# Twenty products in the second group, and the range check moved to ScalarE

## The chip, the core and the metric

The kernel runs on one core of one Trainium2 chip. The metric is the device time of one execution in microseconds: the median of several runs. Before the change it is 560.08 us (three runs, 558.29 to 560.13).

## What is computed

Two blocks stand one behind the other. The first is a gated linear attention: for each of 4 batches and 8 heads a 48 x 48 state is decayed and added to along 768 steps. The second is a two-layer network on its 3072 x 384 result, with SiLU between the layers.

```python
# q, k, v, alpha: (4, 8, 768, 48) float32, alpha between 0.8 and 1
for t in range(S):
    state = alpha[:, :, t, :, None] * state + np.einsum('bhd,bhe->bhde', k[:, :, t], v[:, :, t])
    y[:, :, t] = np.einsum('bhd,bhde->bhe', q[:, :, t], state)
x = y.transpose(0, 2, 1, 3).reshape(3072, 384)
h = x @ w_in                          # w_in: 384 x 2048, float64
out = (h / (1 + np.exp(-h))) @ w_out  # w_out: 2048 x 384, float64
```

The weights come as float64 and are turned into float32 on the chip.

## The kernel before, in words

**Chunks and steps.** The sequence is cut into 24 chunks of 128 tokens (6 along the sequence, 4 batches). The main loop runs 25 steps; step s starts chunk s and ends chunk s - 1. From step 8 on a step has four slots: `scores` of chunk s - 1 (q times k, TensorE; copies out by ScalarE at L806 and L809; masked by GpSimd at L813), `products` of chunk s, `quotient` (both VectorE: scans, transposes), and `values` with `states` of chunk s - 1 (TensorE; ScalarE's copy into `xt` at L851).

**Groups.** Four chunks are a group: 512 tokens, six groups in all, numbered 0 to 5. For each group the network is computed in pieces, which are put between the slots. Pieces are of three kinds:

- `enter_plain(grp, h, pair)`: half the tokens of a group (h) by half of w_in's columns (pair), as ordinary products, four pieces each. ScalarE takes SiLU directly from PSUM (L909).
- `enter(grp, pair)`: all tokens of the group by half of w_in's columns, in seven pieces. It does 20 block products where the ordinary way takes 24, out of sums of blocks: sums of w_in (`sums_w`, 23 for each half, kept in `wx` and in place in `w_in`), sums of xt (`sums_x`, 11 for a group, kept in `xc`), and sums of the results on VectorE (L944), for which ScalarE copies products out of PSUM (L936). SiLU comes last, in place (L941).
- `leave(grp, h)`: the product with w_out, seven pieces, with sums of its own on VectorE (L1033, `side_by_side` at L1019, and the results' at L1042, L1074, L1076, L1085).

Before the change groups 0 and 1 enter by `enter_plain`, groups 2 to 5 by `enter`. `leave` of one group is interleaved with the entry of the next. All products of the entries go through three PSUM banks (`ps_m`), those of `leave` through two (`ps_o`), attention's through three (`ps_a`).

**Order.** `fill(step, slot)` runs after each slot. It computes how many pieces are due at this slot, linearly between marks, and runs them. Each engine's instructions are put in order by a scheduling layer; matmuls are kept in the program's order after the start, and so are the instructions marked `keep_in_program_order`. Sums of w_in for half 0 run in `leave(0, 1)`, for half 1 in `leave(1, 0)`, four after each piece.

**The range check.** The method divides by running products of alpha and converts the weights by bit operations, so the kernel checks that alpha is at most 1 and that the exponents of the weights lie in a range, and falls back on a general version if not. The generator `audit` loads each input once more: 9 pieces of alpha (128 x 1024), 12 of w_in, 16 of w_out (8-byte words), all through one buffer `bits` of the pool `look`. SP issues the loads (L675, L677); VectorE takes the maximum, and for weights the minimum too, into `seen` (L685), 65 reductions. A call to the generator reduces the piece in the buffer and issues the next load. It is called in every second slot from step 15, and what is left runs with the last pieces after the main loop. At the end `seen` is reduced to one flag.

The words of the change stand on these lines of before: `audit` L657, `enter_plain` L897, `enter` L917, `done` in `leave` L1050, the list of pieces L1107 to L1136, `go_on` L1141, `fill` L1166.

Of the kernel before, what the change touches and what calls it, by code (L numbers as in the profile page):

```python
# [9 lines left out]
I32 = mybir.dt.int32  # L10
U32 = mybir.dt.uint32
U8 = mybir.dt.uint8
AF = mybir.ActivationFunctionType
ALU = mybir.AluOpType
E = mybir.EngineType
# [340 lines left out]
def quotients(  # L356
# [19 lines left out]
    nc = tc.nc  # L376
# [177 lines left out]
    earlier, later = [(low, 0), (high, 1)], [(low, 1), (high, 0)]  # L554
    ones = consts.tile([128, 1], F32, name="ones")
    gps.memset(ones, 1.0)

    st = [fix.tile([128, NP, 2, D], F32, name=f"st{b}") for b in range(B)]
    for t in st:
# [92 lines left out]


    AW = 1024
    seen = []

    def audit():  # L657


        flat = alpha.rearrange("b h s d -> (b h s d)").rearrange("(p c) -> p c", p=128)  # L660
        todo = [(flat[:, c : c + AW], AW, 0) for c in range(0, flat.shape[1], AW)]
        if wide:
            todo += [(moe_w_in[t * 128 : t * 128 + 128, c : c + 512], 512, 1)
                     for c in range(0, DF, 512) for t in range(NKT)]
            todo += [(moe_w_out[f * 128 : f * 128 + 128, :], HD, 1) for f in range(NFT)]
        for kind in (0, 1):
            n = sum(x[2] == kind for x in todo)
            if n:
                seen.append([fix.tile([128, n], F32, name=f"seen{kind}{i}") for i in range(2)])
        at = [0, 0]  # L670
        for src, n, kind in todo:
            t = late["look"].tile([128, 512, 2], I32, name="bits")
            if kind == 0:
                x = t.rearrange("p n w -> p (n w)")[:, 0:n].bitcast(F32)
                nc.sync.dma_start(x, src)  # L675
            else:
                nc.sync.dma_start(t[:, 0:n, :].rearrange("p n w -> p (n w)"), src.bitcast(I32))  # L677
                x = t[:, 0:n, 1]
            yield
            i = at[kind]  # L680
            at[kind] += 1
            for which, op in ((0, ALU.max), (1, ALU.min)):
                if kind == 1 or which == 0:
                    tc.keep_in_program_order(
                        dve.tensor_reduce(seen[kind][which][:, i : i + 1], x, axis=AX, op=op,  # L685
                                          apply_absolute_value=True))

    xts, xcs = {}, {}

# [198 lines left out]
    def g_tiles(grp, pair):  # L888
        for h in range(2):
            gts[grp, h, pair] = gpool.tile([128, 4, 2, TB], F32, name="g")  # L890
# [6 lines left out]
    def enter_plain(grp, h, pair):  # L897

        if h == 0:
            g_tiles(grp, pair)  # L900
        xt = xts[2 * grp + h]
        for f in range(8 * pair, 8 * pair + 8, 2):
            ps = bank(f // 2 % 3).rearrange("p (e n) -> p e n", e=2)
            for e in range(2):
                for t in range(NKT):
                    pe.matmul(ps[:, e, :], lhsT=w_in[:, t, (f + e) * 128 : (f + e + 1) * 128],
                              rhs=xt[:, t, :], start=(t == 0), stop=(t == NKT - 1))
            q, i = divmod(f, 4)
            act.activation(gts[grp, h, pair][:, i : i + 2, q % 2, :], ps, AF.Silu)  # L909
            if grp == 1 and pair == h == 0:  # L910
                differences(f // 2)
                differences(4 + f // 2)
            if grp > 0 and f % 8 == 6:
                side_by_side(grp, h, pair)
            yield

    def enter(grp, pair):  # L917
        g_tiles(grp, pair)
        halves = [gts[grp, h, pair] for h in range(2)]

        s = [halves[o % 2][:, o // 2] for o in range(8)]
        todo = iter(PRODUCTS)

        def new(i):
            return bank(i).rearrange("p (e n) -> p e n", e=2)

        def add(ps, first=False):
            w, x = next(todo)
            for e in range(2):
                pe.matmul(ps[:, e], lhsT=block_w(w)[:, 2 * pair + e], rhs=block_x(grp, x),  # L930
                          start=(first and e == 0), stop=(e == 1), skip_group_check=True)

        def copy(ps, to=None):
            if to is None:
                to = late["part"].tile([128, 2, TB], F32, name="part")
            act.copy(to, ps)  # L936
            return to

        def silu(h, i):
            x = halves[h][:, i : i + 2]  # L940
            act.activation(x, x, AF.Silu)  # L941

        def tt(to, a, b, op=ALU.add):
            dve.tensor_tensor(to, a, b, op)  # L944

        a, b, c = [new(i) for i in range(3)]
        add(a, True)
        copy(a, s[6])
        add(b, True)
        copy(b, s[2])  # L950
        add(c, True)
        tt(s[6], s[6], copy(c), ALU.subtract)
        yield
        add(a)
        t = copy(a)
        add(b)
        copy(b, s[4])
        add(c)
        copy(c, s[7])
        tt(s[7], s[7], t, ALU.subtract)  # L960
        yield
        add(a)
        copy(a, s[5])
        add(b)
        copy(b, s[3])
        tt(s[5], s[5], s[3])
        add(c)
        copy(c, s[0])
        yield
        add(a)  # L970
        tt(s[4], a, s[4])
        b = new(1)
        add(b, True)
        add(b)
        copy(b, s[1])
        yield
        c = new(2)
        add(c, True)
        tt(s[2], s[2], copy(c), ALU.subtract)
        a = new(0)  # L980
        add(a, True)
        tt(s[6], a, s[6])
        silu(0, 2)
        add(b)
        tt(s[5], copy(b), s[5], ALU.subtract)
        yield
        add(c)
        tt(s[1], c, s[1])
        tt(s[3], s[1], s[3], ALU.subtract)
        a = new(0)  # L990
        add(a, True)
        tt(s[2], a, s[2])
        add(b)
        tt(s[7], b, s[7])
        silu(1, 2)
        yield
        add(c)
        combine(s[1], -1, s[1], -1, s[0])
        tt(s[0], c, s[0])
        silu(0, 0)  # L1000
        a = new(0)
        add(a, True)
        tt(s[3], a, s[3])
        silu(1, 0)
        turn.append(turn.pop(0))
        for h in range(2):
            side_by_side(grp, h, pair)
        yield
# [7 lines left out]
    def side_by_side(grp, h, pair):  # L1016

        x = cells(grp, h, pair, 1, 0)
        dve.tensor_tensor(x, x, cells(grp, h, pair, 1, 1), ALU.add)  # L1019

    def leave(grp, h):
# [26 lines left out]
        steps = iter(range(7))  # L1048

        def done():  # L1050
            if 2 * grp + h in (1, 2):
                sums_w(2 * grp + h - 1, 4 * next(steps) + 4)

        def new(i):
            return out_bank(i, HO)
# [51 lines left out]
    def plain(grp, h, pair):  # L1107
        return (enter_plain(grp, h, pair), 12, 2 * (2 * grp + h) + 2)

    def group(grp):  # L1110
        return [[(enter(grp, pair), 12, GB * grp + GB)] * 7 for pair in range(2)]

    def output(grp):
        return [[(leave(grp, h), 12, GB * grp + GB)] * 7 for h in range(2)]
# [1 line left out]
    def both(x, y):  # L1116
        for i in range(max(len(x), len(y))):
            pieces.extend(x[i : i + 1] + y[i : i + 1])
# [5 lines left out]
    pieces += [plain(1, 0, 0)] * 4 + [(leave(0, 0), 12, GB)] * 7  # L1124
    phases = [len(pieces)]
    pieces += [plain(1, 1, 0)] * 4
    both([(leave(0, 1), 12, GB)] * 7, [plain(1, 0, 1)] * 4 + [plain(1, 1, 1)] * 4)
    phases.append(len(pieces))
    before = output(1)
    for grp in range(2, NG):  # L1130
# [10 lines left out]
    def go_on():  # L1141

        nonlocal done
        next(pieces[done][0], None)
        done += 1

    audits = audit()
    done, bridged = 0, 0
    STEPS = NT + 1
    SLOTS = 4  # L1150
# [15 lines left out]
    def fill(step, slot):  # L1166

        at = step * SLOTS + slot
        if at < marks[0]:
            if at == SLOTS:  # L1170
                next(conv[0])
            elif step >= 1:
                convert(0, (at - SLOTS) * 3 // (marks[0] - SLOTS) + 1)
            return
        i = next(i for i, m in enumerate(marks[1:]) if at < m)
        a, b = [work_at[n] for n in ([0] + phases)[i : i + 2]]
        due = a + (b - a) * (at - marks[i] + 1) / (marks[i + 1] - marks[i])
        if at % 2 == 0 and step > 3 * GB + 2:
            next(audits, None)
        while work_at[done + 1] <= due and pieces[done][2] <= bridged:  # L1180
            convert(0, 3 * (done // 2) + 6)
            convert(1, 3 * (done - 6) // 2)
            go_on()

    for step in range(STEPS):
        if step == 1:
# [28 lines left out]
    while next(audits, 0) is None:  # L1215
        turns += 1
        for _ in range(1 + turns % 2):
            go_on()

    checks = [(least.rearrange("p n j -> p (n j)"), ALU.min, 2.0**-64, ALU.is_gt),  # L1220
              (seen[0][0], ALU.max, 1.0, ALU.is_le)]
    if wide:
        checks += [(seen[1][0], ALU.max, float(1083 << 20), ALU.is_le),
                   (seen[1][1], ALU.min, float(898 << 20), ALU.is_ge)]
    ends = work.tile([128, len(checks)], F32, name="ends")
    for i, (x, op, bound, holds) in enumerate(checks):
        e = ends[:, i : i + 1]
# [71 lines left out]
```

## Time and profile before

| what | value |
|---|---|
| runs | 560.08 us median, 558.29 to 560.13 |
| profiled execution, first to last instruction (span) | 558.1 us |
| its own time outside the span | not given by the page; the fastest run is 0.2 us above the span, the median 2.0 |
| TensorE | 541.4 us busy, 97% |
| VectorE | 445.1 us busy, 80% |
| ScalarE | 208.4 us busy, 37% |
| GpSimd | 75.9 us busy, 14% |
| mean granted TensorE clock | 0.994 |

The page calls TensorE's matmuls PE and its weight loads PEld, VectorE DVE, ScalarE ACT, GpSimd POOL and SyncE SP. A group line gives line, engine, operation, tiles out<-in, shape and count, then after the bar busy time and mean ns of one, then the engine's idle time just before them and what ended most of it. A matmul in float32 is two rows of the trace, so a product of two matmuls is four rows. A waits line reads: engine, what waited, for whom, then total us, times and longest us. In a timeline the columns are start, us, engine, line, operation, and in brackets the idle time before.

### The profile page before, as it was taken

The page shows a single profiled execution, that of the slowest core. Times are in us where ns is not written, and L with a number is a line of the kernel's source. Part 1 is how long each engine was busy: PE and PEld are TensorE (multiplying, and loading weights), DVE is VectorE, ACT ScalarE, POOL GpSimd, SP SyncE. Part 2 cuts the span into 40 slices and gives each one's busy share as a digit, 9 for nine tenths or more (in the row PEclk, how much of TensorE's full clock was granted, in tenths as well). Part 3 has the DMA queues.
Part 4 walks back from the last instruction along what each step waited for, and adds up shares of the span by engine and source line. Part 5 has one row for each costly group of instructions (what it writes and reads, how often), then busy time and mean ns, then how long its engine had stood idle before and what let it go on. Part 6 is the DMA issues. An engine that isn't in the chain of part 4 may idle for free. (4 is left out here: it accounts for less than half of the span.)

```text
span 558.1 us, 12640 instructions
## 1 busy us (share of the span) xinstructions
PE 541.4 (97%) x5026; PEld 488.8 (88%) x5026; DVE 445.1 (80%) x801; ACT 208.4 (37%) x466; POOL 75.9 (14%) x146
## 2 busy tenths in 40 slices
PE   5999999999999999999999999999999999999996
PEld 3788887998899898899999999988998999998996
DVE  5887889974999799997998986998894775857531
ACT  3456643223333243353353353353263341432200
POOL 4100010221211211021021021021121000001000
PEclk9799999999999999999999999999999999999999
DMA  9999861164445525355445654717712122333101
GB/s 218 255 276 177 232 189 40 38 164 108 126 131 136 142 62 134 88 145 157 129 109 142 194 141 115 198 22 179 180 48 84 53 99 95 111 109 106 38 25 32
DMA packets 99220, 70.13 MB, mean 126 GB/s; under 512 B 56272, under 2 KB 88656, under 8 KB 99152
## 3 DMA queue, kind: packets, MB, share of 16 engines
q1 hardware_dynamic: 97232, 65.30, 44.6%
q0 software_dynamic: 1920, 3.93, 2.0%
q8 instruction: 41, 0.67, 0.5%
q14 instruction: 27, 0.22, 0.1%
HBM read 61.34 MB, written 7.86 MB: 124 GB/s over the span
## 5 line engine op out<-in xcount | busy, mean ns | idle before, releaser
L388 PE MATMUL ps_o<-w_out,g 128*128 128x192 f32 x768 | 134.7, 329 | 1.1 <-DVE o L1042 0.9
L388 PEld LDWEIGHTS ps_o<-w_out,g 128*128 128x128 f32 x768 | 125.4, 190 | 5.1 <-DVE o L1042 2.3
L388 PE MATMUL ps_m<-xt,w_in 128*128 128x256 f32 x480 | 113.6, 383 | 1.5 <-ACT xt L851 1.1
L388 PEld LDWEIGHTS ps_m<-xt,w_in 128*128 128x128 f32 x480 | 89.1, 190 | 14.4 <-ACT xt L851 1.6
L388 PE MATMUL ps_o<-wt,g 128*128 128x192 f32 x576 | 99.7, 326 | 0.0
L388 PEld LDWEIGHTS ps_o<-wt,g 128*128 128x128 f32 x576 | 95.1, 190 | 1.6 <-issue 0.2
L388 PE MATMUL ps_m<-xc,w_in 128*128 128x256 f32 x288 | 70.7, 382 | 0.0
L685 DVE TENSOR_REDUCE seen<-bits 128x1 f32<-128x384 int32 (+2 forms) x65 | 42.5, 689 | 24.0 <-DMA bits<-in_moe_w_out_dram 19.6
L388 PEld LDWEIGHTS ps_m<-xc,w_in 128*128 128x128 f32 x288 | 53.6, 190 | 7.0 <-DVE g L944 0.3
L941 ACT ACTIVATE g<-g 128x1024 f32<-128x1024 f32 x32 | 33.0, 1056 | 59.0 <-DVE g L944 59.0
L1033 DVE TENSOR_TENSOR g<-g 128x512 f32<-128x512 f32 x72 | 49.8, 708 | 6.1 <-PE ps_o L388 6.1
L1045 POOL DMA_DIRECT2D out_dram<-o x40 | 22.0, 550 | 223.2 <-DVE o L1042 127.6
L813 POOL TENSOR_SCALAR_AFFINE_SELECT g<-g 64x256 f32<-64x256 f32 x64 | 34.2, 534 | 124.8 <-ACT g L806 105.8
L388 PE MATMUL ps_m<-xc,wx 128*128 128x256 f32 x192 | 50.0, 383 | 1.0 <-DVE xc L586 1.0
L936 ACT COPY g<-ps_m 128x512 f32<-128x512 f32 x64 | 36.5, 588 | 36.5 <-PE ps_m L388 36.4
L388 PEld LDWEIGHTS ps_m<-xc,wx 128*128 128x128 f32 x192 | 35.2, 190 | 5.3 <-ACT u L1064 1.3
L944 DVE TENSOR_TENSOR g<-ps_m,g 128x512 f32<-128x512 f32 x56 | 37.0, 684 | 2.9 <-PE ps_m L388 2.7
L722 DVE TENSOR_TENSOR_SCAN u<-al,one 128x516 f32<-128x516 f32 x24 | 30.0, 1249 | 10.6 <-ACT al L719 10.3
L909 ACT ACTIVATE g<-ps_m 128x512 f32<-128x512 f32 x32 | 19.1, 596 | 42.8 <-PE ps_m L388 42.3
L936 ACT COPY part<-ps_m 128x512 f32<-128x512 f32 x32 | 18.9, 589 | 43.0 <-DVE g L944 21.3
L752 DVE TENSOR_TENSOR_SCAN p<-al,inv 128x516 f32<-128x516 f32 x24 | 29.9, 1246 | 1.0 <-PE ps_a L388 0.4
L388 PE MATMUL ps_a<-g,vn 128*32 128x128 f32 x768 | 27.5, 278 | 1.8 <-POOL g L801 1.7
(126 smaller groups left out, 611.4 us busy)
## 6 DMA issues: line engine op xcount, KB each, us to landing
bits<-in_moe_w_in_dram SPq DMA_DIRECT2D x24, 512.0 KB, 4.8
bits<-in_moe_w_out_dram SPq DMA_DIRECT2D x32, 384.0 KB, 3.1
at<-in_alpha_dram SPq DMA_DIRECT2D x64, 96.0 KB, 2.5
kt<-in_k_dram SPq DMA_DIRECT2D x64, 96.0 KB, 2.5
qt<-in_q_dram SPq DMA_DIRECT2D x64, 96.0 KB, 2.6
bits<-in_alpha_dram SPq DMA_DIRECT2D x9, 512.0 KB, 3.8
out_dram<-o POOLq DMA_DIRECT2D x40, 96.0 KB, 2.4
flips<-turn SPq DMA_DIRECT2D x12, 256.0 KB, 2.4
```

Source lines behind the costliest of these rows:

```text
L388: in_order(nc.tensor.matmul(*args, **kw))
L685: dve.tensor_reduce(seen[kind][which][:, i : i + 1], x, axis=AX, op=op, apply_absolute_value=True))
L722: dve.tensor_tensor_scan(u[:, end - 1 :: -1], sg[:, end:0:-1], one[:, end:0:-1], 0.0, ALU.mult, ALU.add)
L752: dve.tensor_tensor_scan(p[:, 0:end], sg[:, 0:end], iv[:, 0:end], 0.0, ALU.mult, ALU.add)
L813: gps.affine_select(x, x, pattern=[[0, NP], [1, CH]], compare_op=ALU.is_ge, fill=0.0, base=0, channel_multiplier=-1)
L909: act.activation(gts[grp, h, pair][:, i : i + 2, q % 2, :], ps, AF.Silu)
L936: act.copy(to, ps)
L941: act.activation(x, x, AF.Silu)
L944: dve.tensor_tensor(to, a, b, op)
L1033: dve.tensor_tensor(cells(grp, h, pair, *to), cells(grp, h, pair, *x), cells(grp, h, pair, *y), ALU.subtract)
L1045: (gps if grp < NG - 1 else nc.sync).dma_start(out[r : r + C, c * HO : (c + 1) * HO], o)
```

## The change

- In group 1, half 1 of w_in's columns enters by `enter` (20 products) and no longer by two `enter_plain`; `sums_x(1)` is put ahead of it, and it is interleaved with `leave(0, 1)`. Half 0 of group 1 stays plain.
- For that, half 1's sums of w_in run sooner: three after each piece of `leave(0, 0)` once the late buffers are there, four after each piece of `enter_plain(1, 1, 0)`, the rest at the beginning of `enter`. Half 0's run later, in `leave(1, 0)`, and group 2 takes half 1 first.
- `side_by_side` of the plain pieces (sums of g for `leave`) is put on a list and runs one piece later.
- The range check is done by ScalarE: loads are issued on ScalarE's queue; alpha takes two passes (Abs, then Relu of |x| - 1 with its sum into `beyond`), the weights three (Abs of the upper 16 bits, scaled; Abs of 1 minus that; Relu with its sum). One buffer, as before. The generator is called twice in each slot from step 10 on: first pass ahead of the slot's pieces; the other passes and the next load behind them.
- The check covers the pieces of the weights that are not yet fetched when its list is made: 8 of w_in and 16 of w_out, with the 9 of alpha 33, where it was 37.

```diff
@@ audit @@
-        for src, n, kind in todo:
-            t = late["look"].tile([128, 512, 2], I32, name="bits")
-            ...
-                nc.sync.dma_start(t[:, 0:n, :].rearrange("p n w -> p (n w)"), src.bitcast(I32))
-                x = t[:, 0:n, 1]
-            yield
-            ...
-                        dve.tensor_reduce(seen[kind][which][:, i : i + 1], x, axis=AX, op=op,
-                                          apply_absolute_value=True))
+        def step(to, x, func, scale=1.0, bias=0.0, to_sum=None):
+            kw = {} if to_sum is None else {"accum_out": to_sum}
+            tc.keep_in_program_order(act.activation(to, x, func, bias=bias, scale=scale, **kw))
+
+        def begin(kind, src, n):
+            t = late["look"].tile([128, 512, 2], I32, name="bits")
+            ...
+            tc.keep_in_program_order(act.dma_start(to, src))
+            return t
+
+        t = begin(*audited[0])
+        yield
+        for i, (kind, _, n) in enumerate(audited):
+            ...
+            if kind == 0:
+                step(x, x, AF.Abs)
+            else:
+                step(x, t.bitcast(I16)[:, 0:n, 3], AF.Abs, scale=2.0**-14)
+            yield
+            if kind == 1:
+                step(x, x, AF.Abs, scale=-1.0, bias=ones)
+            step(x, x, AF.Relu, scale=1.0 if kind == 0 else 2.0**14 / 944, bias=minus,
+                 to_sum=beyond[:, i : i + 1])
+            if i + 1 < len(audited):
+                t = begin(*audited[i + 1])
+            yield
@@ enter_plain @@
+            if grp == h == 1:
+                sums_w(1, sums_done[1] + 4)
             if grp > 0 and f % 8 == 6:
-                side_by_side(grp, h, pair)
+                owed.append((done, grp, h, pair))
@@ enter @@
+        sums_w(pair, len(SUMS_W))
@@ leave: done @@
-            if 2 * grp + h in (1, 2):
-                sums_w(2 * grp + h - 1, 4 * next(steps) + 4)
+            if grp == h == 0 and late:
+                sums_w(1, sums_done[1] + 3)
+            if grp == 1 and h == 0:
+                sums_w(0, 4 * next(steps) + 4)
@@ the list of pieces @@
+    def second(grp, pair):
+        return [(enter(grp, pair), 12, GB * grp + GB)] * 7
+
     def group(grp):
-        return [[(enter(grp, pair), 12, GB * grp + GB)] * 7 for pair in range(2)]
+        return [second(grp, pair) for pair in ((1, 0) if grp == 2 else (0, 1))]
-    both([(leave(0, 1), 12, GB)] * 7, [plain(1, 0, 1)] * 4 + [plain(1, 1, 1)] * 4)
+    pieces.append((sums_x(1), 0, 2 * GB))
+    both([(leave(0, 1), 12, GB)] * 7, second(1, 1))
@@ go_on @@
+        while owed and owed[0][0] < done:
+            side_by_side(*owed.pop(0)[1:])
@@ fill @@
-        if at % 2 == 0 and step > 3 * GB + 2:
+        if step > 2 * GB + 1:
             next(audits, None)
         while work_at[done + 1] <= due and pieces[done][2] <= bridged:
             ...
+        if step > 2 * GB + 1:
+            next(audits, None)
```

More of the change, by code (lines that the diff above doesn't have):

```diff
@@ L12 @@
 U8 = mybir.dt.uint8
+I16 = mybir.dt.int16
 AF = mybir.ActivationFunctionType
@@ L556, in quotients @@
     gps.memset(ones, 1.0)
+    minus = consts.tile([128, 1], F32, name="minus")
+    gps.memset(minus, -1.0)
     st = [fix.tile([128, NP, 2, D], F32, name=f"st{b}") for b in range(B)]
@@ L654, in quotients @@
     AW = 1024
-    seen = []
+    audited = [(0, c, AW) for c in range(0, B * H * S * D // 128, AW)]
+    if wide:
+        audited += [(1, src, src.shape[1]) for src in list(sources)]
+    beyond = fix.tile([128, len(audited)], F32, name="beyond")
     def audit():
         flat = alpha.rearrange("b h s d -> (b h s d)").rearrange("(p c) -> p c", p=128)
[L661 to L670, printed above, removed]
-        for src, n, kind in todo:
-            t = late["look"].tile([128, 512, 2], I32, name="bits")
+        def step(to, x, func, scale=1.0, bias=0.0, to_sum=None):
+            kw = {} if to_sum is None else {"accum_out": to_sum}
+            tc.keep_in_program_order(act.activation(to, x, func, bias=bias, scale=scale, **kw))
+        def begin(kind, src, n):
+            t = late["look"].tile([128, 512, 2], I32, name="bits")
+            words = t.rearrange("p n w -> p (n w)")
+            to, src = (words[:, 0:n].bitcast(F32), flat[:, src : src + n]) if kind == 0 else (
+                words[:, 0 : 2 * n], src.bitcast(I32))
+            tc.keep_in_program_order(act.dma_start(to, src))
[3 more added lines that the diff above has]
+        for i, (kind, _, n) in enumerate(audited):
+            x = t.bitcast(F32)
+            x = x.rearrange("p n w -> p (n w)")[:, 0:n] if kind == 0 else x[:, 0:n, 0]
@@ L673, in audit @@
             if kind == 0:
-                x = t.rearrange("p n w -> p (n w)")[:, 0:n].bitcast(F32)
-                nc.sync.dma_start(x, src)
-            else:
-                nc.sync.dma_start(t[:, 0:n, :].rearrange("p n w -> p (n w)"), src.bitcast(I32))
-                x = t[:, 0:n, 1]
+                step(x, x, AF.Abs)
+            else:
+                step(x, t.bitcast(I16)[:, 0:n, 3], AF.Abs, scale=2.0**-14)
             yield
[L680 to L685, printed above, removed]
-                                          apply_absolute_value=True))
+            if kind == 1:
+                step(x, x, AF.Abs, scale=-1.0, bias=ones)
@@ L1144, in go_on @@
         next(pieces[done][0], None)
+        while owed and owed[0][0] < done:
+            side_by_side(*owed.pop(0)[1:])
         done += 1
     audits = audit()
+    owed = []
     done, bridged = 0, 0
@@ L1220, in quotients @@
     checks = [(least.rearrange("p n j -> p (n j)"), ALU.min, 2.0**-64, ALU.is_gt),
[L1221 to L1224, printed above, removed]
+              (beyond, ALU.max, 0.0, ALU.is_le)]
     ends = work.tile([128, len(checks)], F32, name="ends")
```

## The prediction

> **What bounds the kernel now.** I read the page first: how full each engine is and what it does.
>
> ```profile
> span 558.1 us, 12640 instructions
> PE 541.4 (97%) x5026; PEld 488.8 (88%) x5026; DVE 445.1 (80%) x801; ACT 208.4 (37%) x466; POOL 75.9 (14%) x146
> L685 DVE TENSOR_REDUCE seen<-bits 128x1 f32<-128x384 int32 (+2 forms) x65 | 42.5, 689 | 24.0 <-DMA bits<-in_moe_w_out_dram 19.6
> ```
>
> TensorE sets the end: idle for 16.7 us of the span, some 6 of them at the start and 4.5 after its last matmul. The L685 line is the range check, 42.5 us of VectorE. Then the waits of TensorE alone: those that a fuller or emptier VectorE can move are about 1 us each.
>
> ```profile
> PE ps_m L388 <- DVE g L944: 1.3, 2, 0.9
> PE ps_m L388 <- DVE xc L586: 1.0, 1, 1.0
> ```
>
> The timeline of TensorE prices the work. A piece of enter_plain is 12 rows and the next piece starts 2.59 us later; a product of enter() is 4 rows, next start 0.87 us later.
>
> ```profile
> 150.00 2.75 PE L388 MATMUL ps_m<-xt,w_in 128*128 128x256 f32 x12
> 152.59 2.76 PE L388 MATMUL ps_o<-w_out,g 128*128 128x192 f32 x16
> 303.51 1.03 PE L388 MATMUL ps_m<-xc,wx 128*128 128x256 f32 x4
> 304.38 1.03 PE L388 MATMUL ps_m<-xt,wx 128*128 128x256 f32 x4
> ```
>
> Busy time by stretch, in those where the changed check will run: scores of chunk 9 to values of chunk 11, then to scores of chunk 14, then to values of chunk 17.
>
> ```profile
> 144.70:189.70 45.00, 45.00 (x525) 40.87 (x521) 41.02 (x75) 14.26 (x43) 9.17 (x16) 1.00 0.54 145
> 189.70:237.40 47.70, 46.35 (x488) 41.68 (x480) 46.96 (x92) 18.13 (x43) 6.21 (x12) 1.00 0.36 94
> 237.40:317.30 79.90, 79.90 (x794) 73.42 (x792) 74.00 (x124) 33.32 (x79) 12.23 (x24) 1.00 0.54 148
> ```
>
> The columns are TensorE, its weight loads, VectorE, ScalarE, GpSimd. ScalarE (14.26 of 45) looks like the place with room. What the shares hide is the time from a check transfer's issue to its landing. The instructions on that buffer, by stretch: alpha before 300 us, the later w_in, w_out after 452 us.
>
> ```profile
> DMA to landing us min/median/max: 3.6/3.8/4.9
> ...
> DMA to landing us min/median/max: 3.4/3.6/4.6
> ...
> DMA to landing us min/median/max: 2.7/2.9/3.2
> ```
>
> At the end, where VectorE has little else, its timeline shows the cost of one buffer with a transfer in series:
>
> ```profile
> 501.70 1.01 DVE L685 TENSOR_REDUCE seen<-bits 128x1 f32<-128x384 int32 x2 [1.90 <-DMA bits<-in_moe_w_out_dram]
> 505.72 1.01 DVE L685 TENSOR_REDUCE seen<-bits 128x1 f32<-128x384 int32 x2 [2.46 <-DMA bits<-in_moe_w_out_dram]
> ```
>
> Reads end at 502.71, the next begin at 505.72: 3.0 us of nothing. Elsewhere before this is hidden, since two slots of work lie between a transfer and its reductions.
>
> [...]
>
> **Products.** Eight pieces (24 products' worth) at 2.59 us become 20 products at 0.87: 20.8 - 17.3 = 3.5 us less of TensorE, on the path.
>
> **VectorE in that stage.** Added: 11 sums of xt at 0.42 (L582), 14 sums of g at 0.68 (L944) and one scalar_tensor_tensor of 0.68, 14.8 us. The 23 sums of w_in and the four side_by_side stay as many; the other pair's sums go to leave(1, 0), in exchange for those that leave it. VectorE is busy 57.4 of the 70 us from 126 to 196: 12.6 idle. The stage is over-filled by 14.8 - 12.6 + 3.5 = 5.7 us, of which about 3.6 fit into the idle time of 112 to 126, where the sums now start. Later VectorE loses 42.5 us of reductions and their 24.0 of idling; TensorE waited for it through them for some 1 us (xc at 369). side_by_side a piece later only takes a wait for the SiLU (L1019 waits 12.0) off VectorE's queue.
>
> **The check on ScalarE.** It now covers nine pieces of alpha, 8 of w_in and 16 of w_out (the list is taken when four are already fetched). Each is a transfer, then 2 passes (alpha) or 3 in place: 9x2 + 24x3 = 90 ACTIVATEs. All use one buffer, so each round runs in series: land, pass, pass, issue again. The built program's order on ScalarE puts little between issue and use; rows at values of chunk 13:
>
> ```
> 204 L675 DMACopy bits<-in_moe_w_in_dram 128x1024 [waits Activation_49]
> 205 L859 TensorCopy xt<-ps_a 128x3x128 [waits PE_49]
> 206 L668 Activation bits<-bits 128x512 [waits DMAHW0_49]
> 207 L668 Activation bits<-bits,ones 128x512 [waits Activation_49]
> 208 L668 Activation bits,beyond<-bits,minus 128x512 [waits Activation_49]
> 209 L675 DMACopy bits<-in_moe_w_in_dram 128x1024 [waits DMAHW5_49,Activation_49]
> ```
>
> Behind row 206 stand the copies out of the three ps_m banks, of ps_o and of the scores. Matmuls into those banks wait for them; GpSimd's selects wait for the scores.
>
> So I add up ScalarE's round: landing + passes + the kernel's own copies that stand outside the shadow of the landing (between the passes, or between the last pass and the next issue, at 0.5 a 512-wide copy, 0.25 a 192-wide, 0.96 a SiLU, 0.4 an xt, 0.2 to 0.3 the small ones: their pitches back to back in the timeline). Landings I take between minimum and median, as the queue is its own: 3.7, 3.8, 2.8. Passes: alpha 1.06 + 1.15 (with pointer); w_in and w_out like the conversion's strided reads at L629, 0.69 and 0.56, and 0.09 more for the two with a pointer: 2.25 and 1.86.
>
> - alpha: 9 x (3.7 + 2.21) + 3.3 = 56.5 (3.3: three 512-wide copies, two xt, four small ones). TensorE's work there: 12 pieces at 2.59, a short one of 1.73, three values at 2.0, two scores at 0.83: 40.5.
> - w_in: 8 x (3.8 + 2.25) + 5.9 = 54.3 (four copies, two SiLUs, two of 192, six small), against 46.4 (47.70 less the stalls in it).
> - w_out: 16 x (2.8 + 1.86) + 10.7 = 85.3 (eleven copies, two SiLUs, three xt, one of 192, seven small), against 79.9.
>
> Sum 196.1 against 166.8: ScalarE is 29.3 us longer. Three banks let TensorE run ahead once by about 3 us; 26.3 stay. None of it is won back, for TensorE has no slack later.
>
> Span: 558.1 - 3.5 - 1.35 (stalls of the second stretch, left out of 46.4) - 1.0 (xc) + 26.3 = 578.6. The median of the runs is 2.0 over the profiled span, so 580.6, **581 us**.
>
> Bounds. Low: shortest landings (3.5, 3.4, 2.7) and passes without price for pointer or sum, overlapping by 0.09: 52.1, 47.5 and 76.6, where TensorE's 79.9 holds; 9.7 us more, 564 in the end. High: longest landings (4.9, 5.0, 3.2), and the sum that Relu leaves costing as much as a one-element ACTIVATE (203 ns at L441): some 60 more, 614. A sum that costs nothing or 0.2 us is all I can say of it; I take nothing. Issuing on ScalarE I put in the landing; SP's took 327 ns each. Thirty-seven issues leave SP, where they waited for the reductions (64.9 us at L677); after the start TensorE waits for no load, so nothing is gained. They share DMA semaphores with SP's loads, so a late ScalarE can hold loads: a loss I leave to the range. The memset of minus is 0.09 us at the start, under a load's 4.0.
>
> **Rivals.**
> - *ScalarE hides its waits, VectorE's stage eats the gain.* For it: ScalarE is idle for two thirds of its time. Against: the issue stands next to the use. 3.5 + 2.35 gained, 2 to 6 lost: about 560.
> - *It is faster.* One mechanism: landings on ScalarE's own queue are short. The rounds equal TensorE's work at (40.5 - 3.3)/9 - 2.21 = 1.9 us for alpha, 2.8 for w_in, 2.5 for w_out; at some 2.4 on the whole the check is free, and VectorE's overflow finds its room. Then 558.1 - 3.5 - 2.35 + 2.0 = 554. Against: nothing landed under 2.7, and alpha under 3.5.
> - *It doesn't do what it says.* The built order has the 20 products and 33 transfers on ScalarE; I give that nothing.
>
> **Numbers.** ScalarE's rounds decide: 0.79, own range 564 to 602. Hidden: 0.10. Faster: 0.11. Under 0.5% (2.8 us) this kernel's measurement can't tell from no change. The range goes from 557 (the hidden case included) to 602, with the fast case and the highest landings left out.
>
> **What would show it.** Right: ScalarE's idle time led by a wait of its first pass for bits, 60 us or more over 33 waits of 1 to 4 us; TensorE waiting on ScalarE for ps_m and ps_a, 20 us or more, all within chunks 9 to 18; before and after that stretch the same pace, group 1 being 3.5 shorter. Wrong: landings near 2 us; or ScalarE idle for TensorE rather than for transfers; or the largest waits of TensorE on VectorE in group 1.

## The result, and the profile after

The changed kernel takes 600.5 us (median of four runs, 599.42 to 603.52) where the kernel before, beside it, took 559.84 (558.29 to 560.13): 1.074 times as long, with a 95% interval of 1.071 to 1.077. The forecast was 581 us, with a range of 557 to 602. The sign holds, and the range by 1.5 us; the size is short by half: +21 us forecast, +41 measured. Ratios and intervals below leave out one run, of the kernel with short passes (614.1 us at a mean clock of 0.906), which fell out of the state of all others.

The page of the kernel after, first the lines that answer to those shown of before. The row of PEclk gives the TensorE clock in 40 slices of the span; the last three lines are the check's transfers (count, KB each, median us from issue to landing).

```profile
span 597.7 us, 12669 instructions
...
PE 552.4 (92%) x5010; PEld 495.4 (83%) x5010; DVE 422.1 (71%) x757; ACT 278.3 (47%) x597; POOL 81.0 (14%) x147
...
PEclk9999999999988879979989999999999999999999
...
L668 ACT ACTIVATE bits<-bits 128x384 f32<-128x384 int16 (+2 forms) x33 | 24.0, 727 | 61.8 <-DMA bits<-in_moe_w_out_dram 27.0
...
bits<-in_moe_w_out_dram ACTq DMA_DIRECT2D x16, 384.0 KB, 3.6
bits<-in_alpha_dram ACTq DMA_DIRECT2D x9, 512.0 KB, 4.4
bits<-in_moe_w_in_dram ACTq DMA_DIRECT2D x8, 512.0 KB, 4.0
```

TensorE has the fewer products (5010 instructions for 5026) and yet is busy for 11 us more; and it is idle for 45.3 us where it was 16.7. The first pass (L668) waited 61.8 us for its transfers.

The same stretches as in the prediction, by what the program does in them:

```profile
143.30:199.60 56.30, 46.81 (x472) 40.90 (x472) 42.57 (x72) 33.15 (x70) 7.64 (x16) 0.91 0.61 168
199.60:236.30 36.70, 30.06 (x264) 26.06 (x264) 29.79 (x61) 22.99 (x46) 8.34 (x5) 0.86 0.57 158
236.30:357.10 120.80, 108.85 (x1065) 97.17 (x1064) 89.43 (x156) 76.71 (x176) 14.76 (x31) 0.96 0.57 161
sum 213.80, PE 185.72 PEld 164.13 DVE 161.79 ACT 132.86 POOL 30.75; mean PE 61.91 PEld 54.71 DVE 53.93 ACT 44.29 POOL 10.25
```

Together 213.8 us, where before took 172.6 (144.7 to 317.3): 41.2 us more. Ahead of it the kernel after stands 1.4 us sooner, and behind it both need the same (240.6 and 240.8 us). So all of the loss lies in the stretch of the check's 33 rounds. In it TensorE is idle for 28.1 us (before: 1.35), and its clock, 1.00 throughout before, is 0.91, 0.86 and 0.96.

Who TensorE waits for, from the list of waits:

```profile
PE ps_a L389 <- DMA kn<-flips: 8.1, 2, 4.6
PE ps_m L389 <- ACT g L947: 5.2, 2, 3.6
PE ps_m L389 <- ACT part L947: 5.1, 5, 1.7
...
PE ps_a L389 <- DVE st L876: 3.4, 1, 3.4
PE ps_a L389 <- ACT xt L859: 3.1, 3, 1.7
PE ps_o L389 <- ACT g L952: 2.6, 1, 2.6
```

The waits for VectorE's g and xc that were shown of before are down to 0.3 us and to nothing. In their place stand ScalarE's copies and SiLUs (16.0 us in the four lines that name ACT), and first of all a transfer, kn, of which the prediction had no word. The 3.4 us for VectorE's st lead back to ScalarE too: shortly before (at 259.50) VectorE had stood 2.25 us for a SiLU of L952 that came behind a pass of the check.

The timeline of ScalarE shows a round:

```profile
181.59 0.33 ACTq L675 DMA_DIRECT2D bits<-in_alpha_dram  x1
185.53 1.06 ACT L668 ACTIVATE bits<-bits 128x1024 f32<-128x1024 f32 x1 [3.97 <-DMA bits<-in_alpha_dram]
186.62 1.15 ACT L668 ACTIVATE bits<-bits,minus 128x1024 f32<-128x1024 f32 x1
187.68 0.19 ACT L668 ACTIVATION_READ_ACCUMULATOR bits<-bits,minus 128x1 f32 x1
```

Issue, 3.97 us of nothing, two passes, and a read of the sum as an instruction of its own. The copy into `part` that TensorE's next product needs ran at 187.77, behind all of it. Here is what TensorE made of three stalls, from its timeline:

```profile
161.34 0.89 PE L389 MATMUL ps_a<-p,kp 48*64 48x128 f32 x30 [1.75 <-ACT xt L859]
...
177.04 0.87 PE L389 MATMUL ps_a<-vn,kn 128*32 128x48 f32 x32 [3.48 <-DMA kn<-flips]
177.84 2.07 PE L389 MATMUL ps_m<-xc,wx 128*128 128x256 f32 x4
...
188.38 1.13 PE L389 MATMUL ps_m<-xc,wx 128*128 128x256 f32 x4 [1.65 <-ACT part L947]
```

After 1.65 us of standing still a product takes 1.13 us, about its usual 1.03. After 3.48 us it takes 2.07. Windows of 1 us show why (length, TensorE's busy time and instructions, granted clock, the DMA engines' share, GB/s):

```profile
175.00:176.00 1.00, 0.00 (x0) 0.95 0.54 145
176.00:177.00 1.00, 0.00 (x0) 0.50 0.79 136
...
183.00:184.00 1.00, 1.00 (x34) 1.00 0.88 271
```

The clock is 0.50 from 175.91 to 182.74, by the trace's record of it. Such slow times followed all five stalls of 2.65 us and more in the check's stretch, and a sixth followed the one of 1.75 us at 161.34, which had another of 0.52 just ahead of it. They begin at 162.26, 175.91, 203.22, 216.87, 261.24 and 309.03 us, each lasts 3.41 or 6.83 us, and from one beginning to the next it is 4, 8, 4, 13 and 14 times 3.41 us. So in this trace the clock changes on a grid of 3.41 us, and none of the six beginnings is that of a stall (the one ahead of 175.91 began at 173.56). Together the six are 30.7 us, in 27.7 of which TensorE was busy, at half its pace: some 13.8 us of work lost, an estimate.

And SP, which issues attention's loads, from its list of waits:

```profile
SPq L487 <- DMA bits<-in_moe_w_out_dram: 30.4, 9, 5.1
SPq L487 <- DMA bits<-in_alpha_dram: 19.9, 5, 4.9
SPq L487 <- DMA bits<-in_moe_w_in_dram: 9.5, 2, 5.6
...
SPq L786 <- DMA bits<-in_alpha_dram: 3.3, 1, 3.3
```

L487 loads q, k and alpha of coming chunks, and has nothing to do with the buffer `bits`. With the lines for L504, L506, L778 and L786 SP stands 85.5 us in wait for the check's transfers; in before its loads at L486 stood 3.9 (the check's own issues, which were on SP there, stood 58.3 for such transfers, but all after 317 us). In the trace all 33 transfers of the check count on the same eight semaphores as SP's. Behind 25 of the 33 the next transfer on that semaphore is one of SP's; all 25 were issued after the landing, 24 of them within 0.06 us of it. Of the 393 transfers of SP and ScalarE in this trace that have a predecessor on their semaphore none was issued before that one had landed. What is late then is kn: of its four loads ahead of the 4.6 us stall the second stood 3.3 us (the last line above), issued at 199.47 where the load of alpha ahead of it on its semaphore landed at 199.46, and ahead of the stall of 3.48 us SP had stood 3.7 for a transfer of alpha. VectorE transposes kn's source into `turn` (`flip`), SP writes that to memory (L778) and, at the next chunk's scores, reads it back turned (L786); TensorE's states need it. The kn loads themselves landed no later than in before (median 2.1 us, there 2.9), so more traffic on the DMA engines does not show in them.

### The profile page after: what moved, and what is told of

Read it like the earlier page. It is cut to its first block, busy times and chain, and to the rows that moved or that the text cites. A ratio compares the mean times of both kernels' runs of the same rounds, so it can differ in the third digit from the quotient of the medians.

```text
span 597.7 us, 12669 instructions
## 1 busy us (share of the span) xinstructions
PE 552.4 (92%) x5010; PEld 495.4 (83%) x5010; DVE 422.1 (71%) x757; ACT 278.3 (47%) x597; POOL 81.0 (14%) x147
## 5 line engine op out<-in xcount | busy, mean ns | idle before, releaser
L389 PE MATMUL ps_m<-xt,w_in 128*128 128x256 f32 x396 | 94.9, 383 | 2.3 <-ACT part L947 1.2
L389 PEld LDWEIGHTS ps_m<-xt,w_in 128*128 128x128 f32 x396 | 73.3, 190 | 14.2 <-ACT part L947 2.0
L389 PE MATMUL ps_m<-xc,w_in 128*128 128x256 f32 x324 | 82.9, 394 | 0.0
L389 PEld LDWEIGHTS ps_m<-xc,w_in 128*128 128x128 f32 x324 | 62.6, 197 | 8.6 <-issue 0.2
L389 PE MATMUL ps_m<-xc,wx 128*128 128x256 f32 x216 | 60.2, 403 | 9.2 <-ACT g L947 5.2
L389 PEld LDWEIGHTS ps_m<-xc,wx 128*128 128x128 f32 x216 | 41.2, 199 | 16.8 <-ACT g L947 5.8
L952 ACT ACTIVATE g<-g 128x1024 f32<-128x1024 f32 x36 | 37.1, 1053 | 36.4 <-DVE g L955 35.0
L668 ACT ACTIVATE bits<-bits 128x384 f32<-128x384 int16 (+2 forms) x33 | 24.0, 727 | 61.8 <-DMA bits<-in_moe_w_out_dram 27.0
L955 DVE TENSOR_TENSOR g<-g,part 128x512 f32<-128x512 f32 x27 | 18.5, 686 | 27.9 <-ACT part L947 19.9
L389 PEld LDWEIGHTS ps_a<-p,kp 48*64 48x64 f32 (+1 forms) x640 | 21.6, 149 | 16.7 <-issue 9.1
L389 PE MATMUL ps_a<-p,kp 48*64 48x64 f32 (+2 forms) x640 | 26.8, 263 | 8.4 <-DVE st L876 3.4
```

Of the source, the lines that this page charges most:

```text
L389: in_order(nc.tensor.matmul(*args, **kw))
L668: tc.keep_in_program_order(act.activation(to, x, func, bias=bias, scale=scale, **kw))
```

## The experiments

**The products alone.** The change, with the check of before on VectorE, loads on SP.

```diff
-        t = begin(*audited[0])
-        ...
+        for src, n, kind in todo:
+            ...
+                nc.sync.dma_start(x, src)
+            ...
+                        dve.tensor_reduce(seen[kind][which][:, i : i + 1], x, axis=AX, op=op,
...
-        if step > 2 * GB + 1:
+        if at % 2 == 0 and step > 3 * GB + 2:
             next(audits, None)
...
-        if step > 2 * GB + 1:
-            next(audits, None)
```

> The change without the moved check: 20 products, sums of w_in and side_by_side as in the change; the check is that of the kernel before (VectorE, loads by SP, from step 15). My theory (the series of landing and passes on ScalarE costs it all): 553 to 560, at most the 3.5 us of the products gained and at least some of it given back to VectorE in group 1. Rival, VectorE over-filled in group 1 is a large part of the loss: 565 or more, with waits of TensorE on VectorE of 5 us or more between chunks 8 and 12.

Measured: 561.02 us (560.4 to 562.31), 1.0038 of before, interval 1.0021 to 1.0055, and 1.0 us over my range. The products' part gains nothing. The stretch from 126 to 232 us (TensorE, its weight loads, VectorE, ScalarE, GpSimd), first of before:

```profile
126.00:232.00 106.00, 103.91 (x1133) 93.04 (x1128) 92.89 (x173) 35.57 (x98) 17.05 (x33) 1.00 0.44 118
```

and of this run:

```profile
126.00:232.00 106.00, 100.59 (x1083) 89.36 (x1085) 100.39 (x190) 41.26 (x105) 19.01 (x34) 1.00 0.45 121
```

In the same 106 us TensorE is busy for 3.3 us less and VectorE for 7.5 us more. Over the span TensorE is busy for 4.0 us less and idle for 5.3 more.

**The check alone.** The kernel before, with `audit` and its calls of the change.

```diff
+        def begin(kind, src, n):
+            ...
+            tc.keep_in_program_order(act.dma_start(to, src))
...
-        if at % 2 == 0 and step > 3 * GB + 2:
+        if step > 2 * GB + 1:
             next(audits, None)
...
+        if step > 2 * GB + 1:
+            next(audits, None)
```

> The kernel before with the check of the change and nothing else. My theory: the loss stands whole, 598 to 608 (the change plus about 3.5 for the products it lacks). If the two parts hurt each other (VectorE late and ScalarE late in the same stretch): 580 to 592.

Measured: 598.66 us, 1.0698 of before (1.0665 to 1.0732), 39.7 us more. ScalarE waits for bits for 65 us. The check makes the whole loss.

**Passes without transfers.** The change, with a load for the first piece of each kind alone: 2 transfers in place of 33, all passes on what lies in the buffer (31 pieces are not checked).

```diff
-            if i + 1 < len(audited):
+            if i + 1 < len(audited) and audited[i + 1][0] != kind:
                 t = begin(*audited[i + 1])
```

> The change with 2 loads instead of 33: one piece of alpha and one of w_in are loaded, all 90 passes run on what lies in the buffer, so the other 31 pieces go unchecked. Landings in series are the cause: 556 to 568. Rival, the passes alone (62 us of ScalarE with their sums) fill ScalarE: 585 or more. Rival, the loads' traffic and the semaphores they share with SP's loads: 556 to 568 too, which the next runs tell apart.

Measured: 564.09 us, 1.0084 (1.0059 to 1.0109). So some 62 us of passes on ScalarE (busy for 275.9 us, with the products alone 214.2) cost 3 us over the products alone (561.02) and 5 over before. TensorE's timeline behind the one load that is left within the rounds shows a loss of that size:

```profile
194.29 0.89 PE L389 MATMUL ps_a<-p,kp 48*64 48x128 f32 x30 [2.71 <-ACT xt L859]
195.12 3.46 PE L389 MATMUL ps_m<-xc,w_in 128*128 128x256 f32 x8
```

One late landing is a stall of 2.71 us and then 3.41 us at half the clock: eight rows in 3.46 us, which at full clock take 1.99.

**Half the pace.** One call to the generator in each slot, not two.

```diff
             go_on()
-        if step > 2 * GB + 1:
-            next(audits, None)
```

> The change with one call of the check in a slot instead of two: the same 33 loads, queue and 90 passes, but a whole slot between a load and its first pass, and the work spread over twice the steps. Landings in series are the cause: 556 to 570, with ScalarE's waits for bits under 25 us. Rival, traffic and shared semaphores: 575 or more, as all loads are there.

Measured: 565.12 us, 1.0125 (1.0092 to 1.0157); ScalarE's waits for bits fall to 24 us. More of the slot's own work now stands between a load and its use. What is left is led by one stall of 3.46 us for kn, and the slow clock after it.

**Transfers without passes.** All 33 loads and waits; the passes over 8 columns.

```diff
-                step(x, x, AF.Abs)
+                step(x[:, 0:8], x[:, 0:8], AF.Abs)
...
+            x = x[:, 0:8]
```

> The change with all 33 loads, waits and passes, but each pass works on 8 columns only (the rest of each piece is not checked). The passes then take some 23 us together and not 70. Theory (landing and passes stand in series on ScalarE, and the sum outgrows TensorE's work): rounds of about 4 + 0.7 give alpha 9 x 5.1 + 3.3 = 49 against 40.5, w_in 45 against 46.4, w_out 79 against 79.9: 562 to 575 us, ScalarE still waiting 60 us or more for bits. Rival (the transfers themselves do it, by what they take from SP's loads and the 16 engines): nothing of that has changed, 590 or more.

Measured: 1.0555 times before (1.052 to 1.059), in four runs of 585.6 to 592.75 us; the profiled one is the fastest, with a span of 583.8. My theory misses: ScalarE waits 77.6 us for bits, as it had it, but the time is 11 to 18 us above its 575. The rival's 590 is met at its edge, though the passes, which it gave nothing, are worth some 10 us against the change whole. TensorE's waits say why:

```profile
PE ps_a L389 <- DMA kn<-flips: 14.1, 3, 10.0
PE ps_a L389 <- ACT xt L860: 4.3, 3, 2.3
PE ps_m L389 <- ACT g L948: 2.9, 3, 1.5
```

ScalarE's own lateness has shrunk (9.0 us with ps_o's 1.8), and a second way takes its place: SP, which stands 83 us in wait for bits, brings kn as much as 10 us late. My theory, one chain on ScalarE, was not enough. There are two ways from a check transfer to TensorE: through ScalarE's order and through SP's.

**The loads on SP.**

```diff
-            tc.keep_in_program_order(act.dma_start(to, src))
+            nc.sync.dma_start(to, src)
```

> The change with its 33 loads issued by SP and no longer on ScalarE's queue. Theory (landing in series with the passes, whoever issues): the round stays as long or longer, since an SP issue waits in line and for ScalarE's last pass: 595 to 612 us. Rival (the queue of its own is the trouble, by semaphores shared between two queues): under 588.

Measured: 603.82 us, 1.0755 (1.0721 to 1.0788). The number is that of my theory, the way is the other one. TensorE's largest wait and SP's:

```profile
PE ps_a L389 <- DMA kn<-flips: 37.6, 7, 9.6
...
SPq L675 <- ACT bits L668: 55.4, 20, 5.3
```

Here SP stands behind ScalarE's passes, seven kn come late, and TensorE's waits for ScalarE's copies are gone but for 1.1 us, although ScalarE itself waits 61.7 us for bits, as in the change. The queue of its own hardly changed the time: it moved the lateness from SP to ScalarE.

**Two buffers.** 288 x 8 bytes each for one of 512 x 8, and each load issued a round ahead; alpha in 16 pieces, of the weights' pieces 288 columns (the rest is not checked).

```diff
+        t, ahead = begin(*audited[0]), begin(*audited[1])
...
-            if i + 1 < len(audited):
-                t = begin(*audited[i + 1])
+            t = ahead
+            if i + 2 < len(audited):
+                ahead = begin(*audited[i + 2])
...
-        late.update(look=pool("look"),
+        late.update(look=pool("look", 2),
```

> The change with two buffers of 288 x 8 bytes for one of 512 x 8, each load issued a round ahead: alpha in 16 pieces of 576 columns, of each piece of the weights the first 288 columns only, 40 rounds for 33. Theory (a landing stands in ScalarE's order ahead of the next pass): it now lands behind another round's passes and copies, ScalarE's waits for bits fall under 20 us and the time to 558 to 570 us. Rival (the transfers and the shared semaphores hold SP, and SP holds TensorE): 580 us or more, with SP's waits for bits still above 60 us.

Measured: 566.89 us, 1.0109 (1.0083 to 1.0135). ScalarE still works 62 us more than in before, but hardly waits. The lines for its waits for bits and for TensorE's for kn:

```profile
ACT bits L668 <- DMA bits<-in_alpha_dram: 3.3, 3, 1.3
...
PE ps_a L389 <- DMA kn<-flips: 6.0, 3, 4.6
```

With the landing behind other work, 35 of the 41 us are gone (566.89 - 561.02 = 5.9 are left). The pieces are smaller as well (288 KB), but that alone can't be it: they landed little sooner (medians of 3.6 us for alpha, 4.0 and 3.0 for the weights). SP still waits 53.9 us for bits; what reaches TensorE is 6.0 us for kn, 4.6 of it in one stall, and half the clock after that.

**Sums of w_in on GpSimd.** The products alone, with the additions and subtractions of `sums_w` moved off VectorE.

```diff
-                combine(block_w(to)[:, r], sa, block_w(a)[:, r], sb, block_w(b)[:, r]))
+                combine(block_w(to)[:, r], sa, block_w(a)[:, r], sb, block_w(b)[:, r], gps))
```

> The products' part of the change with the check of before on VectorE (as in the first run), and the additions and subtractions among the sums of w_in (not those with a factor) moved from VectorE to GpSimd. Theory (the 3.5 us less of TensorE were eaten by VectorE, too full in group 1): VectorE gets some of its time back, TensorE's waits for it shrink, 555.5 to 559 us. Rival (GpSimd is too slow for them, or comes late with its own masks): 561 us or more.

Measured: 568.1 us, 1.0125 (1.0103 to 1.0148): a miss. The sum of the line below took 0.94 us there, and 0.42 on VectorE in before (L582, the same tiles):

```profile
L586 POOL TENSOR_TENSOR w_in<-wx,w_in 128x256 f32<-128x256 f32 x8 | 7.5, 935 | 0.5
```

VectorE waits 5.2 us for such sums, and TensorE once for 2.91 us on VectorE, with a slow clock after it. This neither shows nor refutes that VectorE eats the products' gain; the run with short sums of g, below, does.

**Nearly no check.** The change, with one piece of alpha from step 15 on (both calls to the generator).

```diff
+    audited = audited[:1]
...
-        if step > 2 * GB + 1:
+        if step > 3 * GB + 2:
             next(audits, None)
```

> The change with the range check cut down to a single piece of alpha, at step 15: no check worth the name on any engine, so the most that any placing of it could leave. Theory (the 3.5 us less of TensorE are eaten in group 1, where VectorE is too full before the check begins): TensorE stands at the same places from 140 to 230 us as with the products alone, and only the later waits for VectorE and the end get shorter: 556 to 560 us. Rival (VectorE freed of 65 reductions lets the products win what they are worth): 555 us or less.

Measured: 560.01 us, 0.9992 of before, interval 0.998 to 1.0004. This is the most that any placing of the check could leave of this change: no gain. TensorE stands for VectorE at 143.58, 161.18, 198.50, 219.47 and 230.82 us (1.14, 1.32, 0.98, 1.06 and 0.40), nearly where it does with the products alone.

**Two buffers, begun at step 15.** Both calls to the generator wait for that step.

```diff
-        if step > 2 * GB + 1:
+        if step > 3 * GB + 2:
             next(audits, None)
```

> The two buffers of the seventh run (576 columns of alpha, 288 of each piece of the weights), the check begun at step 15 in place of step 10, 40 rounds in 40 slots. Theory (what two buffers leave is the transfers of the check that hold SP, so that kn comes late for TensorE, in the stage in which VectorE writes its source late anyway): after that stage kn has room, the stall of 4.6 us goes, and the slow clock behind it: 558 to 562 us. Rival (what is left is ScalarE's passes, wherever they stand): 565 us or more.

Measured: 562.63 us, 1.0045 (1.0029 to 1.0062), 0.6 above the range. The stall for kn is gone, and so is the slow clock behind it: the three products of four rows behind that of kn at 170.66 take 1.13, 1.03 and 1.03 us. SP's waits for bits are 34.9 us, and TensorE has none for kn. So it is the stage, not the passes as such; beyond the kernel with nearly no check only 2.6 us are left.

**Short sums of g.** The kernel with nearly no check, and the 14 sums of g in group 1's entry over 8 columns.

```diff
+            if grp == 1:
+                to, a, b = to[:, :, 0:8], a[:, :, 0:8], b[:, :, 0:8]
             dve.tensor_tensor(to, a, b, op)
```

> The ninth run's kernel (the change with one piece of check) and the 14 sums of g in the entry of group 1 done over 8 columns only, so that the results of group 1 are not what the reference has: VectorE has some 8 us less in the stage in question and all else stays. Theory (VectorE, too full in group 1, eats the 3.5 us of the products): TensorE's waits for VectorE of 4.9 us between 140 and 231 shrink to 1 to 3, 556 to 558.5 us against 560. Rival (something else holds the end, whatever VectorE does there): within 0.7 us of the ninth run's 560.

Measured: 557.29 us, 0.9951 of before (0.9933 to 0.997), where the kernel with nearly no check has 0.9992: 2.3 us less. From 126 to 232 us:

```profile
126.00:232.00 106.00, 102.64 (x1176) 91.44 (x1172) 97.07 (x194) 41.60 (x106) 19.51 (x35) 1.00 0.46 121
```

In these 106 us VectorE is busy for 3.2 us less than there (100.23), TensorE for 1.9 us more (100.70), and its waits for VectorE in the stage fall from 4.9 us to 2.5. So VectorE's stage holds a part of the products' gain back. Against the kernel before with nearly no check (0.9967, next), though, the products then gain only some 0.9 of their 3.5 us.

**Before, with nearly no check.**

```diff
+        todo = todo[:1] + todo[-1:]
         for kind in (0, 1):
```

> The kernel before with the range check cut down to one piece of alpha and one of w_out, on VectorE as before: what the check costs the kernel before, and so the most that its move could bring. Theory (it is hidden on VectorE but for a wait of TensorE of 1.0 us for xc and a little at the end): 557.5 to 560 us where before has 559 to 561. Rival (VectorE's 42.5 us of reductions cost TensorE several us): 556.5 us or less.

Measured: 558.52 us, 0.9967 (0.9954 to 0.998). Taking 62 of VectorE's 65 reductions away is worth 1.5 us. That was all that moving them could win.

## Why the prediction was right in sign, and short by half

**ScalarE's rounds in series: right as a mechanism.** "The issue stands next to the use", and ScalarE's idle time is led by its first pass's wait for bits: 62 us in 31 waits, forecast 60 or more in 33. TensorE's waits for ScalarE's copies and SiLUs are 16 us where I had 20 or more, and kn's 8.1 come on top. TensorE was idle for 28.1 us in the stretch; the sum said 26.3. That closeness is partly luck, since two of its terms were off: landings of 4.4, 4.0 and 3.6 us (medians) where I took 3.7, 3.8 and 2.8 ("between minimum and median, as the queue is its own"), which over 9, 8 and 16 rounds is 20.7 us more, and the read of the sum that Relu leaves, 0.19 us 33 times, 6 us where I took nothing. Copies in the shadow of the landings took most of this back: ScalarE's busy time and its waits for bits in the stretch come to 194 us, the sum to 196.1. The passes were priced right to within 0.02 us a round, 0.09 us for a pointer included: 1.06 and 1.15 us for alpha, 0.69, 0.77 and 0.77 for w_in, 0.56, 0.65 and 0.66 for w_out (means of L668). The kernels with two buffers, with half the pace and without transfers show that the landing in the path makes the loss: all passes without it cost 5 us at most.

**The step that failed: TensorE's work was taken as fixed** ("Sum 196.1 against 166.8"). The forecast's stretch is 166.8 of work and 26.3 of idling, 193.1 us; it took 213.8. Of the 20.7 us between them 1.8 are idling, and 18.9 are work: TensorE was busy for 185.7 us (before's 171.25 less 3.5 would be 167.7). The six slow times are 13.8 us of that. How the rest falls into this stretch I can't say, but over the whole span nothing of it is left: 552.4 - 13.8 = 538.6 us of busy time, where the products alone and nearly no check, with the clock full in the stretch, have 537.4 and 538.7. ScalarE, at 194 of 213.8, is not busy or waiting for transfers all the time: the rest is mostly waits for VectorE and TensorE. My sum put 26.3 us of idling into the stretch and priced the work at the clock of before, 1.00. In the trace a clock of 0.50, for 3.41 or 6.83 us, follows wherever TensorE stood idle for 2.09 us or more (at most 2.70) of a step of 3.41 us. That 600.5 us still lies within the range is luck: its top allowed for long landings and a costly read of the sum, not for a slow clock.

**The step left to the range: semaphores shared with SP.** "A late ScalarE can hold loads" was the right fear, and I had put no number to it: 85.5 us of SP's waits, of which 8.1 reach TensorE through kn, with two of the six slow times behind them. In the kernel with short passes this way leads, and with the loads on SP it is nearly the only one. How the 41 us divide between the two ways can't be said, for when one is eased the other gets longer. No run gave the two queues semaphores of their own, so this way is read from the waits in the traces and not tested by itself.

**Products: 3.5 us less, and not one of them gained.** The price is right (TensorE busy for 4.0 us less; by the pitches given it would be 20.7 - 17.4 = 3.3), and so is the term for VectorE, "over-filled by 5.7 us, of which about 3.6 fit". The failed step is that its rest was left out of the sum, where it stood only in the rival "2 to 6 lost": 5.3 us of idling, measured. With it the products are worth +1.3 us of span (+2.1 by medians) in place of -3.5. Short sums of g show the cause for 2.3 us of it.

**VectorE's relief: right.** Forecast 1.0 us for xc, and nothing won back later; the kernel before without its reductions gains 1.5.

**The rivals.** *Hidden, about 560*: the value of the kernel with nearly no check, so half of this rival, VectorE's stage, was true beside the other. *Faster, 554*: no transfer of the check landed in under 3.1 us, and even with no check at all there is no gain to be had. *It doesn't do what it says*: the page has all 33 transfers on ScalarE's queue.

The sum once more, as measured: the check alone costs 39.7 us, the products alone 2.1, and the whole change 40.7.

## What to carry to other kernels

Before moving work to an engine with idle time, look at what stands next to it in that engine's order: a load issued behind one use and awaited by the next puts its whole landing ahead of everything that engine does for others, however low its share of busy time; a second buffer with the load a round ahead took away 35 of 41 us here. When a forecast puts stalls of 2 to 4 us on TensorE, price a slow clock after them too: here 3.41 us at half pace, or 6.83, six times. And ask of each transfer with which others it shares a semaphore: here SP, whose loads have nothing to do with the check, stood 85.5 us for the check's transfers.

## What the runs showed of the hardware that was not expected

- In the change's trace every time at one granted clock between 8.66 and 595.75 us lasts a whole number of steps of 3.41 us, those at 0.50 one or two. From 30 to 590 us all six steps at full clock in which TensorE stood idle for 2.09 to 2.70 us were followed by half clock, and no other, the longest idle time among them being 1.98; in before's trace no step there has over 1.21, and the clock stays at 1.00. A stall's length alone does not tell: 2.28 us (short passes, 229.84 to 232.12) left the clock at 1.00, where an edge at 231.05, by count eight steps behind that of 203.74, cuts it into 1.21 and 1.07; and 1.72 us (sums on GpSimd, 161.05 to 162.77), all within one step, were followed by 0.50 from 163.88 to 167.30, while 1.98 us in one step of the change were not.
- In the change's trace the sum of each of the 33 Relu passes is read by an instruction of its own, ACTIVATION_READ_ACCUMULATOR, 185 to 225 ns.
- A sum or difference of two 128x256 float32 blocks took 0.73 to 1.08 us on GpSimd (sums on GpSimd, L586, L588 and L590) and 0.41 to 0.47 on VectorE (before, L582, L584 and L586; means by tiles).
